# Windowed attention and ResMLP on one core: a rewrite of the transposes, the scores, the sinks and the order of the work

## Chip, cores and metric

One core of a Trainium2 chip runs the whole program. The metric is the device time of one execution in microseconds (us). The kernel before takes 421.32 us, the median of 2 runs (421.09 and 421.56).

## What is computed

Four batches, eight heads, 768 positions, head dimension 64. Each query sees its last 128 positions and the first four ("sinks"). The attention output, 768 x 512 per batch, is the input of a residual block: a mixing over tokens, then a two-layer MLP of width 2048. Inputs and output are float32.

```
scores = scale * q @ k.T
keep   = (col < 4) | ((0 <= row - col) & (row - col < 128))
a      = softmax(where(keep, scores, -1e9))
x      = (a @ v) as [batch, 768, 512]
u      = x + lam * (w_tok @ (alpha1 * x + beta1))
out    = u + lam * (relu((alpha2 * u + beta2) @ w_ch1) @ w_ch2)
```

## The kernel before

The positions of a batch are cut in six blocks of 128. Names: `b` is the batch, `r` a block of queries, `hp` a pair of heads.

Attention (`emit_attention`). q and k come in float32 by sixteen transfers a batch on SP's queue (L155, L156), 256 bytes a row; v comes by eight on POOL's queue, which turns it to float16 on the way (L148). For each of the four head pairs and six blocks, TensorE transposes q and k in float32 against `iden32` (L169, L170) and DVE copies the result as float16 to `qkT` (L171). Then for each block and pair: up to three score matmuls a head, keys of block 0, r-1 and r against 128 queries (L189), all into `pS`; an exponential on ACT (L195); a multiplication with a 0/1 mask on DVE (L196); up to three value matmuls a head, 65 columns of which the last is the sum of the weights (L200); a reciprocal (L207) and one scaling per head (L210). After the last pair of a block DVE makes `xh`, x times lam times alpha1 in float16 (L215). The whole block 0 is a key block for every r, though only its first four rows count.

Dense work (`queue_moe`). A list of closures: six `tok` steps (six matmuls of 512 columns, L231, one for beta1, L235, an addition, L240; every second step transposes u in float32, L244 and L246, and ACT copies it, L248); then for each half of 384 positions 16 `mlp1` steps (four matmuls of 384 columns, L262, ReLU on ACT, L267) and three `mlp2` steps (16 matmuls of 512 columns, L276, an addition, L281, and the store, L282).

Order. The attention of batch b+1 is written out, and `pump(n)` inside it takes n closures of batch b from the list: one after each pair's transposes, two after each (block, pair). So the dense work of a batch is fed between attention steps, and what is left runs at the end. A tile scheduler may still order each engine's instructions by its own rules. Before the loop come batch 0's attention and the preparation of the weights: w_tok is transposed (L301 to L303), w_ch1 is scaled by alpha2 on DVE (L333), w_ch2 by lam on POOL (L339), and beta2 is folded into a bias (L325).

PSUM: four buffers "one" serve transposes and all dense results, two double-size buffers "two" serve `pS`.

Of the kernel before, what the change touches and what calls it, by code (L numbers as in the profile page):

```python
# [7 lines left out]
FP32 = mybir.dt.float32  # L9
# [6 lines left out]
def kernel(  # L16
# [32 lines left out]
    assert window == 128 and 0 < n_sink <= 128, (n_sink, window)  # L49
    assert S % 128 == 0 and D == 64 and H % 2 == 0  # L50

    const = ctx.enter_context(tc.tile_pool(name="const", bufs=1))
    wpool = ctx.enter_context(tc.tile_pool(name="wpool", bufs=1))
    apool = ctx.enter_context(tc.tile_pool(name="apool", bufs=2))
    qkv = ctx.enter_context(tc.tile_pool(name="qkv", bufs=2))
    epool = ctx.enter_context(tc.tile_pool(name="epool", bufs=4))
    spool = ctx.enter_context(tc.tile_pool(name="spool", bufs=4))
    xpool = ctx.enter_context(tc.tile_pool(name="xpool", bufs=2 * NR))
    mpool = ctx.enter_context(tc.tile_pool(name="mpool", bufs=2))
    ps = ctx.enter_context(tc.tile_pool(name="ps", bufs=1, space=bass.MemoryType.PSUM))  # L60

    iden32 = const.tile([P, P], FP32, tag="iden32", name="iden32")
    iden16 = const.tile([P, P], FP16, tag="iden16", name="iden16")
    for iden in (iden32, iden16):
        nc.gpsimd.memset(iden, 0.0)
        nc.gpsimd.affine_select(
            out=iden, in_=iden, compare_op=ALU.not_equal, fill=1.0,
            base=0, pattern=[[-1, P]], channel_multiplier=1,
        )

    mask_r0 = const.tile([P, 2, 128], FP16, tag="mask_r0", name="mask_r0")
    mask_r1 = const.tile([P, 2, 256], FP16, tag="mask_r1", name="mask_r1")
    mask_r2 = const.tile([P, 2, 384], FP16, tag="mask_r2", name="mask_r2")
    for m in (mask_r0, mask_r1, mask_r2):
        nc.gpsimd.memset(m, 1.0)
    nc.gpsimd.affine_select(
        out=mask_r0, in_=mask_r0, compare_op=ALU.is_ge, fill=0.0,
        base=0, pattern=[[0, 2], [1, 128]], channel_multiplier=-1,
    )
    nc.gpsimd.affine_select(  # L80
        out=mask_r0, in_=mask_r0, compare_op=ALU.is_ge, fill=1.0,
        base=-n_sink, pattern=[[0, 2], [0, 128]], channel_multiplier=1,
    )
    nc.gpsimd.affine_select(
        out=mask_r1[:, :, 0:128], in_=mask_r1[:, :, 0:128], compare_op=ALU.is_ge,
        fill=0.0, base=-1, pattern=[[0, 2], [-1, 128]], channel_multiplier=1,
    )
    nc.gpsimd.affine_select(
        out=mask_r1[:, :, 0:128], in_=mask_r1[:, :, 0:128], compare_op=ALU.is_ge,
        fill=1.0, base=-n_sink, pattern=[[0, 2], [0, 128]], channel_multiplier=1,  # L90
    )
    nc.gpsimd.affine_select(
        out=mask_r1[:, :, 128:256], in_=mask_r1[:, :, 128:256], compare_op=ALU.is_ge,
        fill=0.0, base=0, pattern=[[0, 2], [1, 128]], channel_multiplier=-1,
    )
    nc.gpsimd.affine_select(
        out=mask_r2[:, :, 0:128], in_=mask_r2[:, :, 0:128], compare_op=ALU.is_ge,
        fill=0.0, base=n_sink - 1, pattern=[[0, 2], [0, 128]], channel_multiplier=-1,
    )
    nc.gpsimd.affine_select(  # L100
        out=mask_r2[:, :, 128:256], in_=mask_r2[:, :, 128:256], compare_op=ALU.is_ge,
        fill=0.0, base=-1, pattern=[[0, 2], [-1, 128]], channel_multiplier=1,
    )
    nc.gpsimd.affine_select(
        out=mask_r2[:, :, 256:384], in_=mask_r2[:, :, 256:384], compare_op=ALU.is_ge,
        fill=0.0, base=0, pattern=[[0, 2], [1, 128]], channel_multiplier=-1,
    )
    masks = {1: mask_r0, 2: mask_r1, 3: mask_r2}

    lam_b = const.tile([P, DM], FP32, tag="lam_b", name="lam_b")  # L110
    nc.sync.dma_start(lam_b, moe_lam.unsqueeze(0).to_broadcast([P, DM]))
    a1_b = const.tile([P, DM], FP32, tag="a1_b", name="a1_b")
    nc.sync.dma_start(a1_b, moe_alpha1.unsqueeze(0).to_broadcast([P, DM]))
    la1_b = const.tile([P, DM], FP32, tag="la1_b", name="la1_b")
    nc.vector.tensor_mul(la1_b, lam_b, a1_b)

    b1_row = const.tile([1, DM], FP32, tag="b1_row", name="b1_row")
    nc.sync.dma_start(b1_row, moe_beta1.unsqueeze(0))
    lb1_row = const.tile([1, DM], FP16, tag="lb1_row", name="lb1_row")
    nc.vector.tensor_mul(lb1_row, b1_row, lam_b[0:1, :])  # L120
    ones_col = const.tile([P, 1], FP16, tag="ones_col", name="ones_col")
    nc.vector.memset(ones_col, 1.0)

    alpha2_c = const.tile([P, NC], FP32, tag="alpha2_c", name="alpha2_c")
    nc.sync.dma_start(alpha2_c, moe_alpha2.rearrange("(c p) -> p c", p=P))
    beta2_c = const.tile([P, NC], FP16, tag="beta2_c", name="beta2_c")
    nc.gpsimd.dma_start(beta2_c, moe_beta2.rearrange("(c p) -> p c", p=P))

    pending: list = []

    def pump(n: int = 1):
        for _ in range(n):
            if not pending:
                return
            pending.pop(0)()
# [180 lines left out]
    w1f = []  # L316
# [66 lines left out]
```

## Time and profile before

| what | value |
|---|---|
| median of 2 runs | 421.32 us |
| profiled execution, first to last instruction (span) | 422.7 us |
| busy: TensorE matmuls / weight loads | 348.5 / 183.2 us |
| busy: DVE / ACT / POOL | 199.4 / 158.2 / 65.5 us |
| moved by DMA | 28.33 MB in 83839 packets, 77153 of them under 512 B |

The profile's span is all that is shown of that execution's own time. PE is TensorE, PEld its weight loads, which overlap its matmuls. The profile says of itself that matmuls are pipelined and their ends modelled; the pace is therefore read from where the next ones start, not from the mean duration.

### The profile page before, as it was taken

What the parts mean: (1) busy time and instruction counts of PE and PEld (TensorE: products, weight loads), DVE (VectorE), ACT (ScalarE), POOL (GpSimd) and SP (SyncE); (2) the same over time, 40 slices, a digit from 0 to 9 for tenths busy, and PEclk for the clock granted to TensorE, in tenths of its full rate; (3) what the DMA queues carried; (4) which work ended last, traced back from release to release, by engine and by line L of the source; (5) the groups of instructions that cost most, each with busy time, mean ns of one, the idle gap of its engine ahead of it and who ended that gap; (6) DMA issues with size and microseconds to landing.
All of it is one profiled execution on the core that took longest, in us unless ns stands there. A gap on an engine that the chain in (4) does not pass through costs nothing.

```text
span 422.7 us, 6213 instructions
## 1 busy us (share of the span) xinstructions
PE 348.5 (82%) x2424; PEld 183.2 (43%) x2424; DVE 199.4 (47%) x592; ACT 158.2 (37%) x293; POOL 65.5 (15%) x94
## 2 busy tenths in 40 slices
PE   0603558496899999957999999879999999799996
PEld 0302335352445455424555455435554553345552
DVE  1402757975744456445734365567353664310101
ACT  1000344232228268120257284211671852146260
POOL 9621469305100000131000000230000000000000
PEclk9999998557599999965999999969999999699999
DMA  8999995159630010297700100480001002000101
GB/s 144 172 210 213 220 185 76 12 127 122 53 74 2 25 51 2 59 145 97 149 2 2 70 6 26 69 57 0 2 0 51 26 2 76 0 0 2 74 2 74
DMA packets 83839, 28.33 MB, mean 67 GB/s; under 512 B 77153, under 2 KB 79969, under 8 KB 83810
## 3 DMA queue, kind: packets, MB, share of 16 engines
q1 hardware_dynamic: 54450, 19.41, 20.3%
q0 software_dynamic: 29360, 8.52, 19.3%
q8 instruction: 19, 0.31, 0.3%
q14 instruction: 10, 0.08, 0.1%
HBM read 30.15 MB, written 6.29 MB: 86 GB/s over the span
## 4 chain that ended last, share of the span: by engine, by line
PE 70%; DVE 11%; DMA 8%; issue 4%; SPq 3%; ACT 2%; POOL 0%
PE h_ps L262 21%; PE ch_ps L276 19%; PE tok_ps L231 9%; PE pS L189 6%; DMA qknat<-in_k_dram 5%; PE pS L200 4%; PE tr_ps L169 3%; DVE eT L196 3%; DVE xh L215 2%; PE tok_ps L235 2%; PE tr_ps L170 2%; DVE qkT L171 2%; SPq L155 2%; DVE w1f L333 2%; PE uT_ps L246 2%
## 5 line engine op out<-in xcount | busy, mean ns | idle before, releaser
L195 ACT ACTIVATE eT<-pS 128x768 f16<-128x768 f32 (+2 forms) x96 | 66.9, 703 | 202.8 <-PE pS L189 195.1
L262 PE MATMUL h_ps<-uT,w1f 128*128 128x384 f16 x512 | 92.2, 327 | 0.3
L276 PE MATMUL ch_ps<-w2f,hT 128*128 128x512 f16 x384 | 87.2, 379 | 0.0
L267 ACT ACTIVATE hT<-h_ps,bias1c 128x384 f16<-128x384 f32 x128 | 74.0, 581 | 17.8 <-PE h_ps L262 12.1
L169 PE MATMUL tr_ps<-iden,qknat 128*128 128x128 f32 x96 | 34.1, 391 | 38.1 <-DMA qknat<-in_q_dram 26.4
L196 DVE TENSOR_TENSOR eT<-eT,mask_r 128x768 f16<-128x768 f16 (+2 forms) x96 | 49.3, 517 | 26.0 <-ACT eT L195 22.6
L262 PEld LDWEIGHTS <-w1f 128*128 128x128 f16 x512 | 46.9, 98 | 31.4 <-issue 0.5
L171 DVE CAST qkT<-tr_ps 128x256 f16<-128x256 f32 x96 | 36.9, 416 | 38.9 <-PE tr_ps L170 28.6
L148 POOL DMA_DIRECT2D vf<-in_v_dram x32 | 26.4, 840 | 182.3 <-DVE rec L207 165.4
L276 PEld LDWEIGHTS <-hT 128*128 128x128 f16 x384 | 36.0, 98 | 40.8
L281 DVE TENSOR_TENSOR x<-x,ch_ps 128x512 f32<-128x512 f32 x24 | 16.5, 688 | 70.6 <-PE ch_ps L276 70.6
L210 DVE TENSOR_SCALAR x<-pS,rec 128x64 f32<-128x64 f32 x192 | 45.4, 278 | 6.1 <-issue 2.6
L189 PE MATMUL pS<-qkT 64*128 64x128 f16 x480 | 40.0, 238 | 8.2 <-DVE x L210 8.2
L231 PE MATMUL tok_ps<-xh,wtokT 128*128 128x512 f16 x144 | 42.2, 427 | 4.0 <-DVE xh L215 2.5
L200 PE MATMUL pS<-vf,eT 128*128 128x65 f16 x480 | 34.4, 207 | 8.0 <-DVE eT L196 7.6
L207 DVE RECIPROCAL rec<-pS 128x2 f32<-128x2 f32 x96 | 15.7, 167 | 45.5 <-PE pS L200 44.1
L169 PEld LDWEIGHTS tr_ps<-iden,qknat 128*128 128x128 f32 x96 | 16.5, 178 | 47.0 <-issue 28.5
L200 PEld LDWEIGHTS <-eT 128*128 128x128 f16 x480 | 24.4, 105 | 26.3 <-DVE eT L196 23.0
L189 PEld LDWEIGHTS <-qkT 64*128 64x128 f16 x480 | 18.4, 99 | 37.2 <-issue 15.3
L170 PE MATMUL tr_ps<-iden,qknat 128*128 128x128 f32 x96 | 31.5, 361 | 3.2 <-DMA qknat<-in_k_dram 3.2
L240 DVE TENSOR_TENSOR x<-x,tok_ps 128x512 f32<-128x512 f32 x24 | 16.4, 687 | 24.2 <-PE tok_ps L235 24.2
L248 ACT CAST uT<-uT_ps 128x256 f16<-128x256 f32 x48 | 14.4, 389 | 23.1 <-PE uT_ps L246 22.9
(46 smaller groups left out, 179.8 us busy)
## 6 DMA issues: line engine op xcount, KB each, us to landing
qknat<-in_q_dram SPq DMA_DIRECT2D x32, 192.0 KB, 4.5
qknat<-in_k_dram SPq DMA_DIRECT2D x32, 192.0 KB, 4.6
out_dram<-x SPq DMA_DIRECT2D x24, 256.0 KB, 2.0
vf<-in_v_dram POOLq DMA_DIRECT2D x32, 96.0 KB, 4.6
w1f<-in_moe_w_ch_dram POOLq DMA_DIRECT2D x4, 512.0 KB, 13.8
w2f<-in_moe_w_ch_dram POOLq DMA_DIRECT2D x16, 128.0 KB, 4.5
wnat<-in_moe_w_tok_dram POOLq DMA_DIRECT2D x6, 192.0 KB, 6.1
lam_b<-in_moe_lam_dram SPq DMA_DIRECT2D x1, 256.0 KB, 3.9
```

The source lines that it names most:

```text
L169: nc.tensor.transpose(pt[:, 0, :], nat[:, 0, r], iden32)
L170: nc.tensor.transpose(pt[:, 1, :], nat[:, 1, r], iden32)
L171: nc.vector.tensor_copy(tT[:, :, r * P : (r + 1) * P], pt)
L189: nc.tensor.matmul(pS[:, e, t * P : (t + 1) * P], tT[rows, 1, jb * P : (jb + 1) * P], tT[rows, 0, r * P : (r + 1) * P], start=True, stop=True,
L195: nc.scalar.activation(eT[:, :, 0:W], pS[:, :, 0:W], AF.Exp, scale=scale)
L196: nc.vector.tensor_mul(eT[:, :, 0:W], eT[:, :, 0:W], masks[nb][:, :, 0:W])
L200: nc.tensor.matmul(pS[:, e, 384 : 384 + D + 1], eT[:, e, t * P : (t + 1) * P], vf[h][:, jb, 0 : D + 1], start=(t == 0), stop=(t == nb - 1),)
L210: nc.vector.tensor_scalar_mul(xt[:, h * D : (h + 1) * D], pS[:, e, 384 : 384 + D], rec[:, e],)
L231: nc.tensor.matmul(ptok, wtokT[si][:, ti * P : (ti + 1) * P], xh[si], start=(si == 0), stop=False,)
L262: nc.tensor.matmul(ph, w1f[c][:, fi * P : (fi + 1) * P], uT[c][:, n0 : n0 + NTOK], start=(c == 0), stop=(c == NC - 1),)
L267: nc.scalar.activation(hT[chk][:, fi, :], ph, AF.Relu, bias=bias1c[:, fi : fi + 1])
L276: nc.tensor.matmul(pch, hT[chk][:, fi, nt * P : (nt + 1) * P], w2f[fi], start=(fi == 0), stop=(fi == NF - 1),)
```

## The change

The kernel is rewritten with the scheduler in its manual mode, so that every engine executes in the order in which the code is written. Its parts:

- Loads. All go by SP's queue in float32: q and k per head pair with 1536 bytes a row (positions 6p to 6p+5 on partition p), v per block, the weights in pieces of 0.8 to 1 MB through two buffers `wst`. The casts to float16 are engine work: q and k on POOL (in batch 0 every second one on DVE), v on POOL, w_tok and w_ch1 on ACT, w_ch2 times lam on DVE and POOL in halves.
- Transposes of q, k, w_tok and u are in float16, six to a PSUM tile, one DVE copy of 768 columns for six.
- Scores. A tile holds four heads and a key block j against 256 queries, blocks j and j+1; one exponential and one mask multiplication of 1024 columns. The eleventh tile, j = 5, holds all eight heads with 128 queries.
- Sinks. The four sink keys of two heads stand in a block-diagonal matrix `ks`; one matmul of 512 columns a pair gives the scores of queries 256 to 767. Their values stand block-diagonally in `vs`, filled by eight small transfers, and enter by one matmul of 260 columns per block and group of four heads.
- Normalisation: one reciprocal of 4 and one multiplication of 256 columns per four heads; `xh` is two POOL operations per block, the second adds lam*beta1, so the beta1 matmuls go. beta2 is added, and alpha2 multiplied, where u's transposes leave PSUM, so the bias of ReLU goes.
- Order. `dense(b)` returns 66 slots: 0 to 4 `tok`, 5 and 6 transposes of u, 7 `tok`, 8 to 25 `mlp1` with two more transposes of u (12, 14), 26 to 41 `mlp1`, 42 to 65 quarters of `mlp2`. A list `seq` of 34 items for batch b+1 (a first cast, eight transposes, the sinks, 24 attention steps) is laid over the slots: 26 to 60 in batch 0, 4 to 57 in batches 1 and 2. Casts of v are hung on the first six items. The attention of batch 0 runs ahead of all that, with the preparation of w_tok written into it.
- PSUM: three buffers "d" (transposes, dense results), two double-size "S" (scores), one "pv".

```diff
-                nc.tensor.transpose(pt[:, 0, :], nat[:, 0, r], iden32)
-                nc.tensor.transpose(pt[:, 1, :], nat[:, 1, r], iden32)
-                nc.vector.tensor_copy(tT[:, :, r * P : (r + 1) * P], pt)
+    ctx.enter_context(tc.manual_schedule())
...
+    def load_qk(b, hp, t):
+        nat = sb.tile([P, 2, NR * D], FP32, tag="nat", bufs=6, name=f"nat{b}_{hp}_{t}")
+        src = (q, k)[t][b, 2 * hp : 2 * hp + 2]
+        nc.sync.dma_start(nat, src.rearrange("h (p r) d -> p h (r d)", p=P))
...
+    def trans(b, hp, t):
...
+        src = n16.pop((b, hp, t))
+        pt = ps.tile([P, NR, P], FP16, tag="d", bufs=3, name=f"tp{b}_{hp}_{t}")
         for r in range(NR):
+            nc.tensor.transpose(pt[:, r, :], src[:, r, :], iden)
+        nc.vector.tensor_copy(
+            qkT[b][:, 2 * hp + t, :].rearrange("p (i r) -> p r i", r=NR), pt)
...
+    def scores(b, j, G):
+        w = 2 * P if j < NR - 1 else P
+        hps = (2 * G, 2 * G + 1) if j < NR - 1 else tuple(range(HP))
+        pS = ps.tile([P, 2, len(hps), w], FP32, tag="S", bufs=2, name=f"S{b}_{j}_{G}")
+        for i, hp in enumerate(hps):
+            for e in range(2):
+                rows = slice(64 * e, 64 * e + 64)
+                nc.tensor.matmul(
+                    pS[:, e, i, :],
+                    qkT[b][rows, 2 * hp + 1, j * P : (j + 1) * P],
+                    qkT[b][rows, 2 * hp, j * P : j * P + w],
+                    start=True, stop=True,
+                )
...
+        nc.scalar.activation(eT, pS, AF.Exp, scale=scale)
...
+        nc.vector.reciprocal(rec, po[:, :, D:D1])
+        nc.vector.tensor_mul(
+            x[:, 4 * G : 4 * G + 4, :], po[:, :, 0:D], rec.to_broadcast([P, 4, D]))
...
+            nc.gpsimd.tensor_mul(tmp, xf, la1_b)
+            nc.gpsimd.tensor_add(xh, tmp, lb1_b)
...
+            side[20].append(lambda: (cast_w2(0), load_w2(2)))
+            side[24].append(lambda: (cast_w2(1), load_w2(3)))
+            side[28].append(lambda: cast_w2(2))
+            side[32].append(lambda: cast_w2(3))
...
+            lo, hi = (4, ns - 8) if b else (26, ns - 5)
+            for i, c in enumerate(seq):
+                pos = lo + (hi - lo) * i // len(seq)
+                side[pos].append(c)
+                if i < NR:
+                    side[pos].append(mk_v(i))
```

An attention step is one of two kinds, in turn: the scores and exponential of tile i, or the mask of tile i followed by the value matmuls and normalisation of tile i-1.

Place one, ACT at the start of the program, before. `eT` are exponentials (block, pair), `wtokT` copies of transposed w_tok.

```order
L195 ACTIVATE eT_0_3_351<-pS_0_3_352 128x2x128
L195 ACTIVATE eT_1_0_366<-pS_1_0_367 128x2x256
L303 COPY wtokT<-wT_ps_0_767 128x2x128
L303 COPY wtokT<-wT_ps_2_771 128x2x128
L303 COPY wtokT<-wT_ps_4_775 128x2x128
L303 COPY wtokT<-wT_ps_0_781 128x2x128
```

The same place in the change: `E` are exponentials, `wt` the casts of w_tok from the landed `wst`.

```order
L191 ACTIVATE es_224<-sk_219 128x512
L207 ACTIVATE E_0_0_231<-S_0_0_226 128x1024
L409 CAST wt_0_233<-wst_t_147 128x1536
L207 ACTIVATE E_0_1_268<-S_0_1_263 128x1024
L409 CAST wt_1_270<-wst_t_149 128x1536
L207 ACTIVATE E_1_0_315<-S_1_0_310 128x1024
L409 CAST wt_2_332<-wst_t_251 128x1536
```

ACT, which reached w_tok after the fifth exponential, now has one third of w_tok, and so one transfer, ahead of each of its second to fourth score tiles.

Place two, SP's queue while batch 0's dense work runs, before (the end of batch 1's loads and the start of batch 2's; w_ch2 was on POOL's queue).

```order
L155 DMA qknat1_3_309<-in_q_dram 128x6x64
L156 DMA qknat1_3_309<-in_k_dram 128x6x64
L155 DMA qknat2_0_1164<-in_q_dram 128x6x64
L156 DMA qknat2_0_1164<-in_k_dram 128x6x64
L155 DMA qknat2_1_1169<-in_q_dram 128x6x64
```

The same queue in the change, from the row behind the second quarter of w_ch2 on (`nat1` and `vnat1` are batch 1's q, k and v, `wst_w2` quarters of w_ch2).

```order
L64 DMA nat1_0_0_693<-in_q_dram 128x2x384
L64 DMA nat1_0_1_695<-in_k_dram 128x2x384
L64 DMA nat1_1_0_697<-in_q_dram 128x2x384
L64 DMA nat1_1_1_699<-in_k_dram 128x2x384
L64 DMA nat1_2_0_701<-in_q_dram 128x2x384
L64 DMA nat1_2_1_703<-in_k_dram 128x2x384
L69 DMA vnat1_0_705<-in_v_dram 128x8x64
L69 DMA vnat1_1_707<-in_v_dram 128x8x64
L69 DMA vnat1_2_709<-in_v_dram 128x8x64
L69 DMA vnat1_3_711<-in_v_dram 128x8x64
L387 DMA wst_w2_2_777<-in_moe_w_ch2_dram 128x4x512
L387 DMA wst_w2_3_807<-in_moe_w_ch2_dram 128x4x512
```

Ten transfers of batch 1, six of q and k and four of v, now stand ahead of the last two quarters of w_ch2.

Place three, POOL while batch 1's q and k are prepared in the change (`n` are casts of q and k, `vf` of v).

```order
L435 TENSOR_TENSOR w2f<-wst_w_1_685,lam_b 128x512 x2
L154 CAST n_1_0_0_822<-nat_0_0_693 128x2x6x64
L154 CAST n_1_0_1_826<-nat_0_1_695 128x2x6x64
L162 CAST vf_94<-vnat_0_705 128x8x64
L154 CAST n_1_1_0_847<-nat_1_0_697 128x2x6x64
L162 CAST vf_96<-vnat_1_707 128x8x64
L435 TENSOR_TENSOR w2f<-wst_w_2_777,lam_b 128x512 x2
L154 CAST n_1_1_1_871<-nat_1_1_699 128x2x6x64
L162 CAST vf_98<-vnat_2_709 128x8x64
L154 CAST n_1_2_0_888<-nat_2_0_701 128x2x6x64
```

The like place of POOL before, where w_ch2 ends and batch 1's v begins (`vf_0` is its first load):

```order
L339 TENSOR_TENSOR w2f_981<-w2f_981,lam_b 128x512
L338 DMA w2f_990<-in_moe_w_ch_dram 128x512
L339 TENSOR_TENSOR w2f_984<-w2f_984,lam_b 128x512
L339 TENSOR_TENSOR w2f_987<-w2f_987,lam_b 128x512
L339 TENSOR_TENSOR w2f_990<-w2f_990,lam_b 128x512
L148 DMA vf_0_270<-in_v_dram 128x6x64
```

Before, v was turned to float16 by the transfer and q and k by DVE's copies behind the transposes; now POOL casts all three ahead of the transposes.

## Rows read from the trace of the kernel before

**Rows 1.** The page, busy time of each engine, share of the span, instructions.

```profile
PE 348.5 (82%) x2424; PEld 183.2 (43%) x2424; DVE 199.4 (47%) x592; ACT 158.2 (37%) x293; POOL 65.5 (15%) x94
```

**Rows 2.** Windows: stretch, length, busy per engine, PEclk, DMA share, GB/s.

```profile
20.00:40.00 20.00, 2.44 (x11) 1.67 (x12) 2.31 (x12) 0.00 (x0) 3.99 (x7) 1.00 1.15 210
...
80.00:100.00 20.00, 17.11 (x147) 9.51 (x147) 16.42 (x57) 7.88 (x10) 2.65 (x4) 0.64 0.47 85
...
180.00:200.00 20.00, 12.32 (x67) 6.37 (x66) 10.01 (x39) 2.41 (x5) 4.92 (x6) 0.58 0.97 127
...
240.00:260.00 20.00, 20.00 (x186) 10.87 (x184) 11.96 (x37) 15.96 (x25) 0.00 (x0) 1.00 0.04 14
...
340.00:360.00 20.00, 18.64 (x143) 8.48 (x140) 10.31 (x31) 7.11 (x11) 0.00 (x0) 1.00 0.11 41
```

**Rows 3.** The chain that ended last: start, length, what, pieces merged.

```profile
195.01 2.72 PE tok_ps L231 x6
...
280.91 2.72 PE tok_ps L231 x6
...
377.09 10.56 PE h_ps L262 x64
387.65 10.36 PE ch_ps L276 x48
...
418.81 0.69 DVE x L281
```

**Rows 4.** Timeline, attention steps inside batch 1's dense work: start, length, engine, line.

```profile
242.73 0.36 PE L200 MATMUL pS<-vf,eT 128*128 128x65 f16 x6
243.03 0.34 PE L189 MATMUL pS<-qkT 64*128 64x128 f16 x4
...
269.33 0.52 PE L189 MATMUL pS<-qkT 64*128 64x128 f16 x12
...
269.77 0.33 PE L169 MATMUL tr_ps<-iden,qknat 128*128 128x128 f32 x1
```

**Rows 5.** Groups by line and shape, whole span: busy, mean ns | idle before.

```profile
L267 ACT ACTIVATE hT<-h_ps,bias1c 128x384 f16<-128x384 f32 x128 | 74.0, 581 | 17.8 <-PE h_ps L262 12.1
L195 ACT ACTIVATE eT<-pS 128x768 f16<-128x768 f32 x64 | 51.3, 808 | 99.6 <-PE pS L189 99.6
...
L196 DVE TENSOR_TENSOR eT<-eT,mask_r 128x768 f16<-128x768 f16 x64 | 38.3, 600 | 16.0 <-ACT eT L195 14.1 <-issue 1.6
...
L339 POOL TENSOR_TENSOR w2f<-w2f,lam_b 128x512 f16<-128x512 f16 x16 | 19.1, 1207 | 10.1 <-DMA w2f<-in_moe_w_ch_dram 10.0
...
L281 DVE TENSOR_TENSOR x<-x,ch_ps 128x512 f32<-128x512 f32 x24 | 16.5, 688 | 70.6 <-PE ch_ps L276 70.6
...
L207 DVE RECIPROCAL rec<-pS 128x2 f32<-128x2 f32 x96 | 15.7, 167 | 45.5 <-PE pS L200 44.1 <-PE tr_ps L170 1.4
...
L195 ACT ACTIVATE eT<-pS 128x512 f16<-128x512 f32 x16 | 9.6, 599 | 20.4 <-PE pS L189 12.8 <-DVE rec L207 7.6
...
L196 DVE TENSOR_TENSOR eT<-eT,mask_r 128x512 f16<-128x512 f16 x16 | 6.8, 422 | 8.5 <-ACT eT L195 8.2
```

**Rows 6.** The same view, POOL's operations with one input, the two sizes.

```profile
L76 POOL TENSOR_SCALAR_AFFINE_SELECT mask_r<-mask_r 128x256 f16<-128x256 f16 x1 | 0.4, 407 | 0.0
...
L66 POOL TENSOR_SCALAR_AFFINE_SELECT iden<-iden 128x128 f16<-128x128 f16 x1 | 0.3, 292 | 0.0
```

**Rows 7.** Timeline, a mask multiplication on DVE beside POOL's multiplications.

```profile
67.27 2.28 POOL L339 TENSOR_TENSOR w2f<-w2f,lam_b 128x512 f16<-128x512 f16 x2
67.57 2.40 DVE L196 TENSOR_TENSOR eT<-eT,mask_r 128x768 f16<-128x768 f16 x1
```

**Rows 8.** Timeline of the start: first transfer issued, first transpose, the third pair's.

```profile
0.81 0.38 SPq L111 DMA_DIRECT2D lam_b<-in_moe_lam_dram  x1
...
9.65 1.09 PE L169 MATMUL tr_ps<-iden,qknat 128*128 128x128 f32 x4 [9.65 <-DMA qknat<-in_q_dram]
...
35.38 1.09 PE L169 MATMUL tr_ps<-iden,qknat 128*128 128x128 f32 x4 [14.26 <-DMA qknat<-in_q_dram]
```

More of the change, by code (lines that the diff above doesn't have):

```diff
@@ new lines @@
+    QK_ORDER = [(hp, t) for hp in range(HP) for t in range(2)]
+    for hp, t in QK_ORDER[:6]:
+        load_qk(0, hp, t)
+    iden = const.tile([P, P], FP16, name="iden")
+    nc.gpsimd.memset(iden, 0.0)
+    nc.gpsimd.affine_select(
+        out=iden, in_=iden, compare_op=ALU.not_equal, fill=1.0,
+        base=0, pattern=[[-1, P]], channel_multiplier=1,
+    )
+    mask0 = const.tile([P, 1, 2 * P], FP16, name="mask0")
+    maskn = const.tile([P, 1, 2 * P], FP16, name="maskn")
+    for m in (mask0, maskn):
+        nc.vector.memset(m, 1.0)
@@ new lines, with attn_core, mk_s, f @@
+    S_ORDER = [(j, G) for j in range(NR - 1) for G in range(2)] + [(NR - 1, None)]
+    PV_ORDER = [(r, G) for r in range(NR) for G in range(2)]
+    def attn_core(b):
+        steps = []
+        sc = {}
+        def mk_s(i):
+            def f():
+                sc[i] = scores(b, *S_ORDER[i])
+            return f
+        def mk_pv(i, masks_of):
+            def f():
+                for m in masks_of:
+                    mask(sc[m], S_ORDER[m][0])
+                if i >= 0:
+                    pv(b, *PV_ORDER[i])
+                    norm(b, *PV_ORDER[i])
+            return f
+        n = len(S_ORDER)
+        for i in range(n):
+            steps.append(mk_s(i))
+            steps.append(mk_pv(i - 1, [i]))
+        steps.append(mk_pv(n - 1, []))
+        steps.append(mk_pv(n, []))
+        return steps
@@ L249, in mk_tok @@
[L249 to L253 removed]
+                        pt, wtokT[:, si, ti * P : (ti + 1) * P], xh_t[b, si],
+                        start=(si == 0), stop=(si == NR - 1),
+                    )
+                xf = x_t[b, ti].rearrange("p h d -> p (h d)")
+                nc.vector.tensor_add(xf, xf, pt)
+                u16[ti] = sb.tile([P, DM], FP16, tag="u16", bufs=4, name=f"u16_{b}_{ti}")
+                nc.scalar.copy(u16[ti], xf)
@@ new lines, with cast_wtok @@
+    wt16 = {}
+    def cast_wtok(w):
+        wt16[w] = sb.tile([P, 2, S], FP16, tag="wt16", bufs=2, name=f"wt16_{w}")
+        nc.scalar.copy(wt16[w], wst.pop(f"t{w}"))
+        for a in range(2):
+            ti = 2 * w + a
+            pt = ps.tile([P, NR, P], FP16, tag="d", bufs=3, name=f"wT{ti}")
+            for si in range(NR):
+                nc.tensor.transpose(pt[:, si, :], wt16[w][:, a, si * P : (si + 1) * P], iden)
+            nc.vector.tensor_copy(wtokT[:, :, ti * P : (ti + 1) * P], pt)
@@ new lines, in cast_w2 @@
+    def cast_w2(i):
+        src = wst.pop(f"w2_{i}")
+        for a in range(4):
+            eng = nc.vector if a % 2 == 0 else nc.gpsimd
+            eng.tensor_mul(w2f[:, 4 * i + a, :], src[:, a, :], lam_b)
+    core[0]()
+    cast_wtok(0)
+    load_wst_t2()
+    cast_v(0, 0, nc.gpsimd)
+    core[1]()
+    core[2]()
+    cast_wtok(1)
+    load_consts()
+    load_v(0, 4)
+    core[3]()
+    cast_v(0, 1, nc.gpsimd)
+    load_v(0, 5)
+    load_w1(0)
+    core[4]()
+    fold_consts()
+    core[5]()
```

536 lines of the change are left out of this document (291 added, 245 removed).

## Prediction

> **What bounds the kernel now.** I read the busy table first. TensorE is busy 82% of the span, every other engine under 50% [rows 1], so the question is how much of that 82% is needed. The windows answer it: where MLP matmuls run (240 to 260, 340 to 360) TensorE stands at 93 to 100% at a granted clock of 1.00; where a batch's token mixing meets the next batch's transposes and first attention steps (80 to 100, 180 to 200) the clock is 0.64 and 0.58 [rows 2]. The chain gives the period: token mixing of one batch starts at 195.01, of the next at 280.91, so a batch costs 85.9 us [rows 3]. And it gives the price of dense work alone, in the last batch: 64 matmuls of 384 columns in 10.56 us, 0.165 each, 48 of 512 in 10.36, 0.216 each [rows 3]. By these a batch's dense work is 36 x 0.216 = 7.8 (token mixing), 128 x 0.165 = 21.1 and 96 x 0.216 = 20.7, together 49.6. The other 36 us of a batch are attention, float32 transposes and waits. Ahead of the first batch there is a long start: the third pair's transposes begin only at 35.38, after 14.26 us of waiting for q [rows 8], in a stretch where the DMA engines are full (share 1.15) at 210 GB/s [rows 2]. The rest follows from these two things, the period and the start.
>
> **TensorE's work after, per batch.** Prices at full clock:
> - Transposes: 48 of q and k, 24 of u, 128 columns in float16. At the dense pace of 0.165 per 384 columns, 0.055 each [rows 3]: 2.6 and 1.3.
> - Scores: 12 matmuls of 64 x 128 took 0.44, from 269.33 to the next start at 269.77 [rows 4], 1536 columns for two halves of the array. A tile now has 1024: 0.29, eleven tiles 3.2.
> - Value matmuls: six of 65 columns from 242.73 to 243.03, 0.05 each [rows 4]. Eight a step, four in block 0, and one of 260 columns (0.11) from block 2 on: 12 steps, 5.3.
> - Sinks: four of 512 columns, 0.9.
>
> Attention is thus 12.0, dense work with u's transposes 50.9, a batch 62.9.
>
> The other engines have room. ACT: an exponential costs 0.808 at 768 columns and 0.599 at 512 [rows 5], 0.82 ns a column, so 1.02 at 1024; eleven of them, 32 ReLUs at 0.581 [rows 5] (18.6) and some 4 of copies make 34. DVE: a mask at 1024 columns by the same step (0.600 against 0.422) is 0.78, eleven 8.6; twelve normalisations, a reciprocal 0.167 [rows 5] and a multiplication that I put at 0.4 (below 0.688, the price of 512 columns), 6.8; the copies behind transposes are bounded by 0.6 (the mask's pace) and 1.0 (that of the addition, 0.688 for 512) for 768 columns, I take 0.95 as they too read PSUM, eight 7.6; twelve additions 8.3, u's eight 4: 35. POOL: twelve two-input operations of 512 columns at 1.207 [rows 5], 14.5; casts of q, k and v, which the trace does not show: by the one-input operation, 0.407 at 256 and 0.292 at 128 [rows 6], 0.86 at 768 and 0.64 at 512; by the two-input one, 2.36 ns a column, 1.81 and 1.21. I take 0.86 and 0.64, since a cast has one input: 8 x 0.86 + 6 x 0.64 = 10.7. POOL then works 25 us of a batch.
>
> The Trainium skill (GPSIMD Engine Reference, section 4.1, Engine selection) says that operations with one input run there roughly at line rate; no run here shows it. By that, an estimate of 0.64 for 768 columns at the page's 1.2 GHz, the sum would be some 3 us lower.
>
> **The start: 54 us.** The first transfer was issued at 0.81, behind constants the first transpose ran at 9.65 [rows 8]. Now q goes first; I put the first tile at 5. Eight tiles of 0.39 MB move at between 183 GB/s (210 at share 1.15) and 373 (41 at 0.11, the large rows of the output) [rows 2]: the last lands between 13 and 21. DVE needs one cast (0.8) and two copies (0.95) for every two tiles, 10.8 in all. Transposes end at about 19. Attention has twelve steps. The value matmuls of a tile stand ahead of the second next scores on TensorE, so two steps cost scores, exponential, mask, values: 0.5 + 1.0 + 0.8 + 0.9 at half clock and some 0.1 at each handover, 3.6; twelve make 22. Into this go the three parts of w_tok, which place one of the order shows ahead of score tiles two to four on ACT: casts of 1536 columns at 0.82 ns, 1.3 each, and six copies on DVE at 0.95, of the 9.6 I count 7. Mask against POOL (below) 4, the last `xh` 2.4: 19 + 22 + 7 + 4 + 2.4 = 54. With all loads at 373 and no mask waits it is 47, with all at 183 about 62.
>
> A mask can be held by POOL: at 67.57 one took 2.40 instead of 0.60, while POOL ran two multiplications from 67.27 to 69.55 [rows 7]. Both `xh` operations now follow every second normalisation, 2.4 us during which the next mask may come. In the start the steps are 1.8 apart, so of six such meetings about 0.7 each is lost, 4. Between dense slots an attention step has two slots or more (1.3 to 1.7) and its successor as much, so I charge nothing there.
>
> The Trainium skill says more (SBUF — State Buffer, section "SBUF: two separate sides"): DVE with two SBUF inputs and a POOL operation that reads SBUF exclude each other for a whole instruction. The row agrees, 2.40 against 0.60. Taken for every meeting, with POOL at work 38% of a batch and a rest of about 1 us, eleven masks lose 4.5 a batch; if nothing hid this the sum would be about 332 instead of 318.
>
> **Batch 0's dense work: 73.4.** To 62.9 come 3 for token mixing that begins at half clock behind a thin start (the levels 0.58 and 0.64 before stood in such stretches), 1.5 for u's transposes, which wait for an addition, an ACT copy and DVE, and 6 for w_ch2. Place two of the order shows ten transfers, 3.4 MB, ahead of its third quarter. They need 9 to 19 us and the quarter itself 3 to 6, from slot 11 on; slot 28, where DVE and POOL wait for it, comes 15 `mlp1` and two transposes later, 10.6 us. So DVE is 1 to 14 us late and the copies of batch 1's transposes stand behind it; TensorE feels it after two more PSUM buffers. I take 6.
>
> **Batches 1 and 2: 67.4 each.** To 62.9 come 1.5 for u, 2 for the second half of `mlp1`, where three ReLUs and an exponential on ACT (2.8) meet three steps and an attention step on TensorE (2.7), and 1 for POOL: place three of the order shows the casts ahead of the transposes, slots 4 to 16, where TensorE has 9.9 us of work and POOL 10.7. The attention ends eight slots (6.9 us) before the batch does, so `xh` (2.4) is covered. Batch 3 has dense work only: 50.9 + 2.6 = 53.5. From the last addition's start to the end of the span it was 422.7 - 418.8 = 3.9 [rows 3], and that stays.
>
> Sum: 54 + 73.4 + 2 x 67.4 + 53.5 + 3.9 = 319.6, against the profiled span of 422.7. The median of the runs lies 1.4 below that span, so 318.2, said as 318.
>
> **Rivals.**
> - Everything late is covered, chance 0.18. The start takes 47, w_ch2 comes in time, ACT and POOL keep pace: 47 + 66 + 2 x 64.5 + 52.5 + 3.9 - 1.4 = 297. For it: large rows moved at 373 GB/s per full share [rows 2]. Against: these were stores in an idle stretch.
> - POOL paces the transposes, 0.14. With casts at 1.81 and 1.21, batches 1 and 2 have 21.7 us of casts in slots with 9.9 of TensorE's work, 11.8 late instead of 1; batch 0 has 26.5, with its four multiplications of w_ch2, where TensorE has 7.9, 18.6 instead of 6; the start 2 more: 318 + 21.6 + 12.6 + 2 = 354. For it: POOL's two-input price [rows 5]. Against: one input [rows 6].
> - Attention is not hidden at all, 0.03: each interleaved batch is 50.9 and an attention as long as the start's (35 from 19 to 54): 54 + 3 x 85.9 + 53.5 + 3.9 - 1.4 = 368. Against: at 240 to 260 the kernel before hides attention steps between MLP matmuls at 100% busy [rows 2, 4].
> - Slower, by the clock, 0.03. If the small matmuls and their waits keep TensorE at its half level, 1.2 GHz, wherever attention is interleaved, each of the 189 us of full-clock work in batches 0 to 2 costs one more: 318 + 189 = 507. It decides from 103 us of such work on. For it: 0.58 and 0.64 where transposes and attention met token mixing [rows 2]. Against: 1.00 where attention met the MLP [rows 2], and 56 of the 66 slots are MLP slots.
>
> **How the numbers follow.** The forecast has 0.62, with a range of its own of 300 to 338. Of the rivals' weight I leave out the slower one, the unhidden one and half of POOL's: 297 to 350. About 2% is what a measurement of this kernel can tell from no change, 413 to 430. Only the clock rival reaches that, or a mixture of the two before it: faster 0.95, within 2% 0.02, slower 0.03.
>
> **What would show it.** Right: token mixing of batches 1 and 2 begins 66 to 69 us apart; granted clock near 1.00 from batch 0's MLP on; first token mixing at 52 to 57; 0.29 per score tile; mask durations over 2 us beside `xh` in the start only. Wrong: transposes waiting for POOL's casts for over 5 us a batch, casts above 1.5 us; a wait of DVE for w_ch2 above 10 us; clock under 0.9 in batches 1 and 2; a period above 75.

## The result, and the profile after

The changed kernel takes 381.75 us (median of 2 runs, 380.73 to 382.78) against 421.32, a ratio of 0.904 with an interval of 0.895 to 0.914. It is faster, as forecast, but 64 us above the 318 forecast and outside the range of 297 to 350. One execution of a kernel below (the step on the read; it is the profiled one) was in a slow state at 340.63 us, so that its median, 336.44 over all four in the expectations, stands at 335.79 here.

The page of the changed kernel, busy time of each engine, answers to [rows 1].

```profile
PE 286.6 (75%) x1956; PEld 144.9 (38%) x1956; DVE 206.8 (54%) x289; ACT 132.5 (35%) x208; POOL 120.9 (32%) x121
```

TensorE lost 62 us of work, and its share fell as well, from 82 to 75%. So something other than TensorE's work now sets the time in some stretches. What that is, the chain that ended last tells (start, length, what, pieces merged); it answers to [rows 3].

```profile
5.32 5.26 DVE qkT L175 x2
...
25.00 5.26 DVE qkT L175 x2
...
70.90 7.20 PE tok L305 x25
...
98.95 6.43 DMA wst_w<-in_moe_w_ch_dram
...
107.77 10.34 DVE qkT L175 x4
...
120.29 7.75 DVE qkT L175 x3
...
165.85 6.49 PE tok L305 x30
...
177.68 2.65 DVE qkT L175
...
183.71 5.28 DVE qkT L175 x2
...
245.30 6.49 PE tok L305 x30
...
257.13 5.21 DVE qkT L175 x2
...
326.13 6.49 PE tok L305 x30
...
377.51 0.69 DVE x L368
```

Two things can be read off it. The starts of token mixing (`tok`) cut the span of 381.1 into its stretches. And in every stretch but the last, which has no transposes of q and k, the chain runs through the copies behind the transposes (`qkT L175`), which the forecast had put beside other work. Against the forecast's terms:

| stretch | forecast | measured |
|---|---|---|
| start, up to the first token mixing | 54 | 70.9 |
| batch 0's dense work | 73.4 | 95.0 |
| batch 1, batch 2 | 67.4, 67.4 | 79.5, 80.8 |
| batch 3 and tail | 57.4 | 55.0 |

The groups by line and shape (busy, mean ns | idle before) say why.

```profile
L175 DVE COPY qkT<-tp 128x768 f16<-128x768 f16 x32 | 84.5, 2774 | 7.7 <-PE tp L174 7.6
...
L207 ACT ACTIVATE E<-S 128x1024 f16<-128x1024 f32 x40 | 40.9, 1022 | 36.4 <-PE S L200 36.3
...
L218 DVE TENSOR_TENSOR E<-E,maskn 128x1024 f16<-128x1024 f16 x32 | 27.4, 857 | 26.9 <-ACT E L207 26.8
L154 POOL CAST n<-nat 128x768 f16<-128x768 f32 x28 | 23.5, 845 | 32.4 <-issue 24.1 <-DMA nat<-in_k_dram 8.3
...
L162 POOL CAST vf<-vnat 128x512 f16<-128x512 f32 x24 | 16.2, 675 | 10.7 <-DMA vnat<-in_v_dram 6.9 <-PE h L345 3.7
...
L415 DVE COPY wtokT<-wT 128x768 f16<-128x768 f16 x6 | 3.3, 558 | 8.3 <-PE wT L414 8.1
```

The first and the last row are the same operation on the same number of elements, from PSUM to SBUF, with the same types: 2.774 us and 0.558. They differ in the order in which they write. The copy of w_tok writes 768 numbers side by side. That of q and k writes with a step: partition p of `nat` holds positions 6p to 6p+5, so neighbouring columns of a transposed block are six places apart in `qkT` (`"p (i r) -> p r i"`). The forecast had 0.95 for each of them. The other rows came close to their prices: 1.02 for the exponential, 0.86 and 0.64 for POOL's casts, and 0.78 for the mask, which took 0.857 on average.

What it does to TensorE is seen in the timeline at the head of batch 1's dense work (start, length, what [idle before, releaser]).

```profile
173.82 2.71 DVE L175 COPY qkT<-tp 128x768 f16<-128x768 f16 x1
...
177.60 5.28 DVE L175 COPY qkT<-tp 128x768 f16<-128x768 f16 x2
...
176.57 0.49 PE L174 MATMUL tp<-iden,n 128*128 128x128 f16 x6 [1.15 <-DVE qkT L175]
...
180.38 2.08 PE L345 MATMUL h<-uT,w1f 128*128 128x384 f16 x6 [2.07 <-DVE qkT L175]
```

The matmuls of `mlp1` wait for a copy that has nothing to do with them: transposes and dense results share the three PSUM buffers "d", and a buffer comes free when the copy has read it. Only 54% of DVE is busy on average, but in this stretch it is the bound. The windows (answering to [rows 2]; stretch, length, busy per engine, PEclk, DMA share, GB/s) show it side by side.

```profile
90.00:110.00 20.00, 7.66 (x58) 4.49 (x56) 9.68 (x6) 4.91 (x10) 11.94 (x12) 0.87 0.98 306
110.00:130.00 20.00, 11.71 (x58) 5.91 (x55) 18.36 (x11) 3.05 (x6) 8.59 (x10) 0.59 0.12 26
...
205.00:225.00 20.00, 20.00 (x165) 9.72 (x164) 9.09 (x22) 13.85 (x24) 8.50 (x6) 1.00 0.01 2
```

From 205 to 225, where attention steps and MLP matmuls alternate and no transposes are left, TensorE is busy throughout at full clock: the interleaving works. From 110 to 130 DVE is busy 18.36 of 20, and 15.92 of that are the copies. From 90 to 110 neither engine is the bound: TensorE is at 38% and DVE at 48%, with the DMA engines full (share 0.98). That is a second loss, in batch 0 alone.

### The profile page after: what moved, and what is told of

Same layout as the page of the kernel before. It is cut to its first block, busy times and chain, and to the rows that moved or that the text cites. A ratio compares the mean times of both kernels' runs of the same rounds, so it can differ in the third digit from the quotient of the medians.

```text
span 381.1 us, 4896 instructions
## 1 busy us (share of the span) xinstructions
PE 286.6 (75%) x1956; PEld 144.9 (38%) x1956; DVE 206.8 (54%) x289; ACT 132.5 (35%) x208; POOL 120.9 (32%) x121
## 4 chain that ended last, share of the span: by engine, by line
PE 56%; DVE 26%; DMA 5%; ACT 3%; SPq 3%; issue 3%; POOL 3%; DVEq 0%; ACTq 0%
PE ch L362 22%; DVE qkT L175 19%; PE h L345 16%; PE tok L305 7%; PE S L200 3%; PE pv L235 2%; DMA wst_w<-in_moe_w_ch_dram 2%; PE pv L227 2%; DMA vnat<-in_v_dram 2%; PE tp L174 1%; PE pv L239 1%; ACT w1f L429 1%; SPq L166 1%; DMA la_b<-in_moe_alpha_dram 1%; DVE w2f L435 1%
## 5 line engine op out<-in xcount | busy, mean ns | idle before, releaser
L345 PE MATMUL h<-uT,w1f 128*128 128x384 f16 x512 | 101.0, 344 | 12.8 <-DVE qkT L175 11.8
L362 PE MATMUL ch<-w2f,hT 128*128 128x512 f16 x384 | 89.9, 379 | 0.0
L175 DVE COPY qkT<-tp 128x768 f16<-128x768 f16 x32 | 84.5, 2774 | 7.7 <-PE tp L174 7.6
L350 ACT ACTIVATE hT<-h 128x384 f16<-128x384 f32 x128 | 61.9, 492 | 74.3 <-PE h L345 73.6
L257 POOL TENSOR_TENSOR tmp<-x,la_b 128x512 f32<-128x512 f32 x24 | 30.9, 1287 | 109.6 <-DVE x L251 109.6
L207 ACT ACTIVATE E<-S 128x1024 f16<-128x1024 f32 x40 | 40.9, 1022 | 36.4 <-PE S L200 36.3
L174 PE MATMUL tp<-iden,n 128*128 128x128 f16 x192 | 19.5, 256 | 42.4 <-DVE n L154 18.9
L218 DVE TENSOR_TENSOR E<-E,maskn 128x1024 f16<-128x1024 f16 x32 | 27.4, 857 | 26.9 <-ACT E L207 26.8
L305 PE MATMUL tok<-xh,wtokT 128*128 128x512 f16 x144 | 35.3, 401 | 2.2 <-POOL xh L258 1.3
L258 POOL TENSOR_TENSOR xh<-tmp,lb_b 128x512 f16<-128x512 f32 x24 | 34.5, 1437 | 1.9
L154 POOL CAST n<-nat 128x768 f16<-128x768 f32 x28 | 23.5, 845 | 32.4 <-issue 24.1
L251 DVE TENSOR_TENSOR x<-pv,rec 128x256 f32<-128x256 f32 x48 | 20.4, 424 | 1.8 <-DVE rec L250 0.2
```

The source lines that it names most:

```text
L154: eng.tensor_copy(o, i)
L174: nc.tensor.transpose(pt[:, r, :], src[:, r, :], iden)
L175: nc.vector.tensor_copy(qkT[b][:, 2 * hp + t, :].rearrange("p (i r) -> p r i", r=NR), pt)
L207: nc.scalar.activation(eT, pS, AF.Exp, scale=scale)
L218: nc.vector.tensor_mul(ev, ev, m.to_broadcast(list(ev.shape)))
L257: nc.gpsimd.tensor_mul(tmp, xf, la1_b)
```

## The experiments

Two theories were tested. Copy: the step of the write costs 2.2 us a copy, and this lies on the path. Queue: batch 0 loses the rest by late w_ch2. All stretches below come from the starts of token mixing in each kernel's chain. A ratio is that of a kernel's time to the kernel before, with a 95% interval behind it.

| kernel | start | batch 0 | 1, 2 | rest | median |
|---|---|---|---|---|---|
| the change | 70.9 | 95.0 | 79.5, 80.8 | 55.0 | 381.75 |
| step on the read (profiled at 340.63) | 58.7 | 91.1 | 67.1, 67.1 | 55.0 | 335.79 |
| blocked loads | 60.9 | 94.3 | 65.7, 65.7 | 55.3 | 343.57 |
| the change, prefetch first | 71.0 | 87.5 | 79.5, 80.9 | 55.2 | 375.71 |
| read step, constants early | 57.4 | 88.8 | 67.1, 67.1 | 55.0 | 337.00 |
| read step, prefetch first | 58.0 | 79.7 | 67.1, 67.1 | 55.1 | 328.66 |
| read step, both orders | 56.8 | 80.0 | 67.1, 67.1 | 55.1 | 325.92 |
| both orders, w_ch2 on DVE | 56.9 | 75.6 | 67.1, 67.1 | 55.3 | 323.39 |
| read step, w_ch2 on DVE | 57.5 | 84.6 | 67.1, 67.1 | 55.3 | 333.50 |
| read step, no w_ch2 | 64.0 | 68.4 | 67.1, 67.1 | 55.2 | 323.63 |

### The step of the copy: four kernels

The first writes side by side by loading in blocks of 128 positions (two transfers a tile, rows of 256 B instead of 1536).

```diff
-        nc.sync.dma_start(nat, src.rearrange("h (p r) d -> p h (r d)", p=P))
+        for e in range(2):
+            nc.sync.dma_start(
+                nat[:, e].rearrange("p (a d) -> p a d", a=6),
+                src[e].rearrange("(a p) d -> p a d", p=P))
...
-            qkT[b][:, 2 * hp + t, :].rearrange("p (i r) -> p r i", r=NR), pt)
+            qkT[b][:, 2 * hp + t, :].rearrange("p (r i) -> p r i", r=NR), pt)
```

> q and k are loaded by blocks of 128 positions (256 bytes a row, two transfers a tile instead of one), so that the copy behind the transposes writes its 128 columns side by side; nothing else changes. Theory S (the copies' writes of 2 bytes every 12 bytes make them slow, and they are the 62 us that the prediction missed): the 32 copies fall from 2.77 us to about 0.56, the price of w_tok's like copies, and the time to 318 to 335 us. Rival D (the order on SP's queue and POOL's pace set the length of the stretches in which the copies stand, the copies only fill them): the copies get short and the time stays above 365 us. Rival L (the small rows of the loads cost what the copies give back): the start gets longer, the time is between 340 and 365 us.

The second keeps the loads and turns the copy round: it writes side by side, and reads PSUM with a step of 128 numbers.

```diff
-            qkT[b][:, 2 * hp + t, :].rearrange("p (i r) -> p r i", r=NR), pt)
+            qkT[b][:, 2 * hp + t, :].rearrange("p (i r) -> p i r", r=NR),
+            pt.rearrange("p r i -> p i r"))
```

> The loads stay as in the change; the copy walks its columns in the order of the positions, so that it writes side by side and reads PSUM with a step of 128 elements (256 bytes). Theory S in its narrow form (only the step of the write to SBUF costs): copies at 0.56 to 1.0 us, time 315 to 330. Theory S in its wide form (any step costs, on either side): copies stay at 2.5 us or more, time within 2% of 381.75. Rival D: time above 365 whatever the copies take.

The third and fourth are the first with two and three neighbouring positions a partition (rows of 512 and 768 B), so that the copy writes with step 2 and 3.

> Two neighbouring positions to a partition: 512 bytes a row, the copies write every second element (4 bytes apart). If a write costs by the 16-byte lines it touches (a line is met four times), the copies stay near 0.6 to 0.85 us and the time is that of the step 1 kernel or a little less. If any step above one costs the same, the copies stand at 2.77 us and the time near 380.

> Three neighbouring positions to a partition: 768 bytes a row, the copies write every third element (6 bytes apart). By 16-byte lines (met two or three times each): 0.6 to 1.0 us a copy, time as at step 2. If the price grows with the step in proportion (2.77 at 6): about 1.4 us, time 335 to 345. If any step costs the same: 2.77 us, time near 380.

The copy's group in each, in the order blocked loads (step 1), step 2, step 3, and step on the read.

```profile
L178 DVE COPY qkT<-tp 128x768 f16<-128x768 f16 x32 | 17.7, 555 | 26.9 <-PE tp L177 26.3
```

```profile
L178 DVE COPY qkT<-tp 128x768 f16<-128x768 f16 x32 | 31.7, 1011 | 15.6 <-PE tp L177 15.6
```

```profile
L178 DVE COPY qkT<-tp 128x768 f16<-128x768 f16 x32 | 44.4, 1436 | 12.2 <-PE tp L177 12.2
```

```profile
L175 DVE COPY qkT<-tp 128x768 f16<-128x768 f16 x32 | 30.1, 952 | 15.7 <-PE tp L174 15.7
```

Blocked loads: 343.57 us (341.68 to 344.66), ratio to before 0.817, 0.813 to 0.820. Step on the read: 335.79 (334.00 to 337.09), 0.798, 0.794 to 0.803. Step 2 and step 3, one execution each: 340.83 and 350.01. The copies fell as the copy theory has it, but the times did not all keep to its ranges: blocked loads missed 318 to 335 and lie where rival L put them (340 to 365, though without the longer start that it named), the read step missed 315 to 330, and step 3 missed 335 to 345. At step 2 neither price named came true: not 0.6 to 0.85 and not 2.77.

Step 1, 2, 3 and 6 cost 0.555, 1.011, 1.436 and 2.774 us. A straight line of 0.11 + 0.444 x step meets all four within 0.02 us: the copy's time goes with the stretch of SBUF that it writes through. On the read side a step of 128 numbers brings it only to 0.952. The main claim of the copy theory holds: with the read step, an edit of one instruction, the time falls by 46 us, and batches 1 and 2 take 67.1 us, where the forecast had 67.4. The chain of that kernel:

```profile
58.70 7.49 PE tok L306 x25
...
149.76 6.49 PE tok L306 x30
...
216.85 6.49 PE tok L306 x30
...
283.94 6.49 PE tok L306 x30
```

Blocked loads make the cheapest copies and the shortest period, 65.7, and yet a longer time than the read step: they move the same bytes in 85399 packets instead of 43926. In the first ten microseconds the DMA engines move 180 GB/s at a share of 1.03, with the read step 246 at 0.77, and the transposes wait for POOL's casts 26.1 us in all against 18.9. That the packets account for the whole difference was not tested by itself. The row size of a transfer and the step of the copy pull against each other, and the read step has both at little cost.

The Trainium skill (SBUF — State Buffer, section Specifications (TRN2)) gives SBUF lines of 16 bytes, full bandwidth from two hits a line on, and a penalty at each cross to a new line. By the two hits, steps of 2 and 3 numbers, 4 and 6 bytes, would cost what step 1 does; the runs do not agree, 1.011 and 1.436 against 0.555. By the penalty, which has no figure there, the price would rise with the lines written through, an estimate of 96, 192, 288 and 576 of them at step 1, 2, 3 and 6; the runs agree in that it rises. The Trainium skill (VectorE: DVE Perf Modes, section Mode 2×_1P) asks for step 1 and 16-bit numbers for two elements a cycle; the drop from 0.952 or 1.011 to 0.555 fits that, the 2.774 at step 6 does not follow from it.

### Batch 0: who holds w_ch2

With cheap copies batch 0 still takes 91.1, and 88.8 in the kernel with early constants below, which has the same order of these transfers. The windows of the first:

```profile
58.00:68.00 10.00, 9.12 (x42) 4.09 (x42) 4.47 (x8) 3.39 (x6) 0.65 (x1) 1.00 0.01 2
...
78.00:88.00 10.00, 6.30 (x45) 3.59 (x43) 3.32 (x3) 4.41 (x9) 6.03 (x7) 1.00 1.05 309
88.00:98.00 10.00, 1.16 (x10) 0.64 (x10) 2.72 (x3) 0.49 (x1) 3.89 (x4) 0.60 0.94 310
```

The DMA engines rest (share 0.01) in the first ten microseconds of batch 0 and are full when DVE and POOL need w_ch2; then TensorE is busy 1.16 of 10 us, and its clock falls (in the kernel with early constants 1.38, at 0.52, in the same window). So the ten transfers for batch 1 were moved to the resting stretch, first in the kernel with cheap copies, then in the change itself.

```diff
-                side[11].append(lambda nb=nb: prefetch(nb))
+                side[0].append(lambda nb=nb: prefetch(nb))
```

> The kernel with the cheap copies (step on the read side; 336.44 us), with one more edit: the ten transfers of batch 1's q, k, v and u are issued at slot 0 of batch 0's dense work instead of slot 11. Theory queue: in the kernel with cheap copies batch 0's dense work takes 91 us where batches 1 and 2 take 67.1, because these ten transfers stand on SP's queue between w_ch2's second and third quarter while the DMA engines had been idle (share 0.01 from 58 to 70); issued at slot 0 they are done before, batch 0 falls to 73 to 78 and the time to 318 to 325. Rival paced: DVE's and POOL's own work on w_ch2 and the casts for batch 1 pace batch 0, whenever the data come; then the time stays at 332 or above.

> The changed kernel with the ten transfers of batch 1 issued at slot 0 instead of slot 11 and nothing else: the copies still write with a step (2.77 us each). If the two losses are separate, the time falls by as much as with cheap copies, from 381.75 to some 366 to 371. If batch 0 is held by the copies whatever the queue does, it falls by under 5 us.

With cheap copies: 328.66 us (328.56 to 331.02), 0.783, 0.780 to 0.786, batch 0 at 79.7. That is 7 us of time, about half of what the theory asked, and between it and its rival; batch 0 missed the 73 to 78. With the stepped copies: 375.71 (374.23 to 376.93), 0.893, 0.890 to 0.897, a gain of 6.0; the intervals of the two ratios just overlap, the executions (380.73 and 382.78 before) do not, and batch 0 goes from 95.0 to 87.5 behind the same start. The gain is smaller than the 11 to 16 expected there, and larger than the 5 of "held by the copies". The order on the queue costs 6 to 7 us of time by itself, which is not the whole.

The windows of the kernel with cheap copies and the transfers first show what is late next.

```profile
78.00:88.00 10.00, 7.24 (x54) 4.22 (x51) 6.62 (x7) 4.84 (x10) 10.00 (x10) 1.00 0.82 285
```

POOL is busy the whole of it: its half of w_ch2's multiplications takes 1.55 each in the kernel with both orders (before, with float16 in, 1.207 [rows 5]), and the casts for batch 1's transposes stand between them. Ahead of that, the constants (five loads, POOL waits for them until 33.7 us in the start) were issued behind the first quarter of v, alone and with the order above.

```diff
+            load_consts()
...
-    load_consts()
```

> The kernel with the cheap copies (336.44 us), with one more edit: the constants, the layer parameters among them, are loaded behind the first quarter of v instead of behind all of v. Theory: POOL waits for them until 33.7 us in the start, and its casts of w_tok and the normalised sums stand behind; the first token mixing comes at 54 to 56 instead of 58.7 and the time falls by 3 to 5, to 332 to 334. Rival: the start is set by its chain of attention steps, and the constants only push v back by their own time: no change within 1.5 us.

> Cheap copies, the constants early and the ten transfers at slot 0 together. If the queue theory and the constants theory both hold, the savings add: 315 to 322 us, the forecast for the change itself. If either falls, 328 or above.

Alone: 337.0 (336.52 to 337.9), 0.802, 0.799 to 0.804, no change. The first token mixing comes at 57.4, 1.3 earlier, which is what the rival says. The chains agree: with the read step that of the start runs through the eight sink transfers on SP's queue, from 23.71 on, the landing of the constants at 33.61 and POOL; with early constants it runs through the attention steps and w_tok's casts, and is hardly shorter. Both: 325.92 (324.37 to 327.89), 0.775, 0.772 to 0.777; the savings do not add to the 315 to 322 asked for, nor is it the 328 or above for a theory that falls. Behind the early transfers the early constants bring 2.7 us (the intervals are apart), where alone they brought nothing. Next, all sixteen multiplications of w_ch2 went to DVE, with both orders and with the change's own order.

```diff
-            eng = nc.vector if a % 2 == 0 else nc.gpsimd
+            eng = nc.vector
```

> The kernel with cheap copies, early constants and the ten transfers at slot 0 (325.92 us), with all sixteen multiplications of w_ch2 on DVE instead of eight on DVE and eight on POOL. There batch 0's dense work still takes 80.0 us, and POOL is busy 10.0 of the 10 us from 76 to 86: its multiplications take 1.55 each, and the casts for batch 1's transposes stand between them. Theory: POOL paces batch 0; 12 us fewer on POOL bring its dense work to 70 to 74 and the time to 316 to 320. Rival: DVE, which gets eight more multiplications of about 0.7, then makes the copies behind the transposes late; the time stays at 323 or above.

> The kernel with cheap copies and the change's own order of transfers (336.44 us; batch 0's dense work 91 us), with all sixteen multiplications of w_ch2 on DVE. If the late data alone holds batch 0 there, it gains under 3 us, 333 to 337. If POOL's work after the data come is on the path, it gains 5 to 9, 327 to 332.

With both orders: 323.39 (321.18 to 325.29), 0.768, 0.765 to 0.771, batch 0 from 80.0 to 75.6; the time misses the 316 to 320 and lies at 323 or above, where the rival put it. With the change's order: 333.50 (333.28 to 336.85), 0.795, 0.791 to 0.799, in the 333 to 337 of "late data alone"; its interval overlaps that of the read step, so it is not told apart from nothing. In the first of the two, this window answers to the one above.

```profile
78.00:88.00 10.00, 7.95 (x65) 4.95 (x64) 8.41 (x11) 4.42 (x9) 2.62 (x3) 1.00 0.77 279
```

POOL's load has become DVE's (8.41 here, 6.31 with both orders alone), but that is not what TensorE now waits for most: the rival named DVE's copies, and from 78 to 97 the longest wait for one is 0.56. The timeline of SP's queue, POOL and TensorE shows a longer one.

```profile
81.09 6.51 SPq L166 DMA_DIRECT2D vs<-vf  x8
87.65 1.07 SPq L69 DMA_DIRECT2D vnat<-in_v_dram  x2
...
91.04 0.80 POOL L162 CAST vf<-vnat 128x512 f16<-128x512 f32 x1 [7.29 <-DMA vnat<-in_v_dram]
...
92.66 0.82 PE L174 MATMUL tp<-iden,n 128*128 128x128 f16 x6 [2.66 <-POOL n L154]
```

The last two blocks of batch 1's v are issued behind w_ch2's last load, which SP issues by 79.94, and eight sink transfers, which hold SP's queue for 6.51 us; POOL waits 7.29 for them with the casts of q and k behind it in its order, and TensorE 2.66 for one of these. No run took these transfers off the queue. Engine work and late data follow one another here: each remedy uncovers the next. So the last kernel asks for the sum of them. It leaves out the loads of w_ch2 and their multiplication by lam; `w2f` is filled with one number at the start, and the matmuls stay.

```diff
+    nc.vector.memset(w2f, 0.01)
...
-            side[6].append(lambda: (cast_w1(2), load_w2(0)))
-            side[10].append(lambda: (cast_w1(3), load_w2(1)))
-            side[20].append(lambda: (cast_w2(0), load_w2(2)))
-            side[24].append(lambda: (cast_w2(1), load_w2(3)))
-            side[28].append(lambda: cast_w2(2))
-            side[32].append(lambda: cast_w2(3))
+            side[6].append(lambda: cast_w1(2))
+            side[10].append(lambda: cast_w1(3))
```

> The kernel with cheap copies and the change's own order of transfers (336.44 us), which leaves out the loads of w_ch2 and their multiplication by lam: w2f is filled with one number at the start, the matmuls on it stay. Theory: all that batch 0's dense work takes over batches 1 and 2 (91 against 67.1) is late w_ch2, through SP's queue, the two staging buffers, DVE and POOL; it falls to 67 to 72 and the time to 313 to 319. Rival: the half clock and the thin start of token mixing, or the casts of batch 1, which are pressed into slots 26 on, hold part of it; batch 0 stays at 76 or above, the time at 322 or above.

323.63 us (321.55 to 325.12), 0.769, 0.765 to 0.773. The time is above the 313 to 319, because the fill took DVE 6.9 us at the start, ahead of its first copy, and the first token mixing came at 64.0 instead of 58.7. The stretch itself answers: batch 0 takes 68.4, inside 67 to 72. In its windows TensorE is busy 96% at full clock:

```profile
64.00:84.00 20.00, 19.12 (x108) 9.90 (x108) 7.40 (x14) 12.52 (x20) 4.94 (x7) 1.00 0.79 218
84.00:104.00 20.00, 19.19 (x158) 11.05 (x157) 10.90 (x17) 12.88 (x26) 4.83 (x7) 1.00 0.00 1
```

So w_ch2 costs batch 0 some 18 to 20 us in the change's order, by its way through the queue and by the work on it: 20.4 by the stretches (88.8 less 68.4), 17.5 by the times (12.2 less, and 5.3 that the fill took in the start). The clock of 0.60 there is a consequence: without the waits it is 1.00. How the 20 split between two staging buffers, queue, POOL and DVE is not settled beyond the steps above; more staging buffers were not tried.

The best version found that computes the whole, with read step, both orders and w_ch2 on DVE, takes 323.39 us, 15% under the change.

## Why the prediction was wrong, step by step

The step that failed is in the forecast's paragraph on the other engines: "the copies behind transposes are bounded by 0.6 (the mask's pace) and 1.0 (that of the addition, 0.688 for 512) for 768 columns, I take 0.95". Measured: 2.774. Both bounding rows are operations that write side by side, and so does the kernel before's own copy of q and k (L171, 0.416 for 256 columns). The copy's write pattern stands in the diff, and no row of before has such a write by DVE, so neither row bounded it. Eight copies at 1.82 us more are 14.6 a batch. The profiles of the change and the read step give 12.2 of it in the start, 12.4 and 13.7 in batches 1 and 2, and 4 in batch 0, which waits for w_ch2 besides: 42 (46 by the medians) of the 61.5 us between the forecast's sum of 319.6 and the span of 381.1. That it lies almost wholly on the path follows from a number that the prediction had for POOL: in the slots of the transposes TensorE has 9.9 us of work. DVE's copies there take 8 x 2.77 = 22.

The second step is "DVE is 1 to 14 us late [...] I take 6". Its size was off, not its place: with cheap copies batch 0 takes 15 us more than the 73.4 (88.8), and leaving w_ch2 out brings it to 68.4. The forecast counted when the data land; it did not count that DVE and POOL, once the data are there, have 16 multiplications at 0.7 to 1.7 us to do in the very slots where the casts and copies for batch 1 are due. Of the 3 us of half clock at the head of batch 0, 1.6 came: the first 25 matmuls of token mixing took 7.20 in the change, and 5.57 in the kernel with the read step and w_ch2 on DVE in the change's order, where the granted clock stood at 1.00. The windows of the change show the switch.

```profile
72.00:74.00 2.00, 2.00 (x6) 0.73 (x5) 0.21 (x1) 0.62 (x1) 0.00 (x0) 0.50 0.00 0
74.00:76.00 2.00, 2.00 (x11) 0.80 (x9) 1.08 (x2) 0.62 (x1) 0.00 (x0) 0.94 0.00 0
76.00:78.00 2.00, 2.00 (x12) 0.94 (x11) 0.98 (x2) 0.99 (x2) 0.00 (x0) 1.00 0.00 0
```

At 0.50, its lower level of 1.2 GHz, TensorE does 6 of these matmuls in 2 us, at 1.00 twice as many.

What held, once the copy is cheap: the period (67.1 against 67.4, as a sum; its additions of 1.5, 2 and 1 were not measured singly), the end of the transposes in the start (19.05 against 19), the casts on POOL, the exponential, the score tile (four matmuls from 210.33 to the next start at 210.65, 0.32 against 0.29), and batch 3 with the tail (55.0 against 57.4, a little less). The start came at 58.7 against 54: its attention, from 19.05 on, took 39.7 instead of 35. The forecast gave no time to the eight sink transfers on SP's queue ahead of the constants (23.71 to 28.82), through which that chain runs; with the constants early, 1.3 of it went.

The rivals. POOL pacing the transposes at 354 is the nearest in number and fell in mechanism: it needed casts of 1.81, they took 0.845. Unhidden attention and the half clock in batches 1 and 2 fell: from 205 to 225 TensorE is full at 1.00. "Everything covered" at 297 fell with the copies and w_ch2. Of masks beside POOL the profile shows some, the longest 1.67 us against a median of 0.69; the 32 rows above at a mean of 0.857 make about 5 us over all batches ((0.857 - 0.69) x 32), where 4 were charged, to the start alone.

The range failed because its ends were taken from the rivals, and the copies entered none of them: a price without a row of its kind had been treated as bounded.

## What to carry to other kernels

Before an on-chip copy is priced by its element count, read the access pattern on its write side: in these kernels a DVE copy of 16-bit numbers cost nearly in proportion to its write step, while the one step tried on the PSUM read, of 128 numbers, cost 0.4 us over no step at all, so put the step on the read. A copy that empties a PSUM buffer shared with dense work came onto the path here where the copies of a stretch exceeded TensorE's work in it (22 us against 9.9), though the engine's share of the whole span was only 54%: compare the two stretch by stretch. And where preparation of a weight is hung into the first batch, count for each slot what the engines have to do there besides waiting for the data; a kernel that leaves the weight out shows the sum of it. Look too at what small transfers stand ahead of a late load on the same queue.

## What the runs showed of the hardware that was not expected

- DVE, 768 float16 numbers a partition from PSUM to SBUF: 0.555, 1.011, 1.436 and 2.774 us with a write step of 1, 2, 3 and 6 numbers; 0.952 with a read step of 128 and the write side by side.
- The same load of q and k in rows of 256 B, blocked, made copies five times as cheap (0.555) and left the kernel 8 us behind the read step with rows of 1536 B.
- POOL's multiplication of 512 columns took 1.207 with float16 in place [rows 5] and 1.55 to 1.70 with float32 in and float16 out beside DVE's; on DVE it took 0.68 alone and up to 1.76 beside POOL's.
- Eight transfers of 0.5 KB, issued one behind another, held SP's queue for 5.11 us in the change (34.76 to 39.87) and 6.51 in the kernel with both orders and w_ch2 on DVE.
